# Loads of V, w1 and w2 issued by ScalarE on a second DMA queue, in an attention decode kernel that streams its cache

## Chip, cores, metric

One Trainium2 chip, one core of it. The metric is the device time of one execution in microseconds, as the median of the runs. The hardware profiler gives, for one execution of its own, a span (first to last instruction of the program) and that execution's device time.

## What is computed

One token of a decoder block: pre-LayerNorm attention over a cached K and V with 32 heads, 32,768 positions and a head width of 128, then a pre-LayerNorm dense block with a Mish activation, both with a residual. Everything is in bf16. Cut to what matters:

```python
# x [1,1,512]; k_cache, v_cache [1,32,32768,128]; wq [512,4096]; wo [4096,512]
q = (layernorm(x) @ wq).reshape(1, 1, 32, 128).transpose(0, 2, 1, 3)
p = softmax(einsum("bhqd,bhkd->bhqk", q, k_cache) * 128 ** -0.5)
o = einsum("bhqk,bhkd->bhqd", p, v_cache)
h = x + o.transpose(0, 2, 1, 3).reshape(1, 1, 4096) @ wo
# w1 [512,1376]; b1 [1376]; w2 [1376,512]
a = layernorm(h) @ w1 + b1
out = h + (a * tanh(softplus(a))) @ w2
```

K and V are 268 MB each; all else together is 11 MB.

## The kernel before

The cache of one head is read in two halves of K and two of V. Each half is one DMA of 4 MB: 128 partitions, and on each of them 128 consecutive positions of 128 numbers (32 KB). They land in `ring`, six slots of 4 MB: slots 0 and 1 for the halves of K, 2 and 3 for those of V, 4 and 5 for wq and wo. Later w1, w2 and the last rows of wo (`WL`) share slot 4. The last half of V, V(31,1), comes in four pieces. At the start the first K goes to V's slots, and the last head's V(31,0) to K's slot 0, as nothing else wants them (`HOMES`, `AFTER`).

A head's K is worked on in groups of eight tiles of 128 positions. PE transposes the eight tiles into PSUM (L539), VectorE copies them to SBUF (L542), and PE multiplies each by the query (L517), up to three groups later. From the 256 columns of scores VectorE takes the maximum (L579), two small matmuls spread it (L585, L590), and ScalarE forms the exponentials with their sum in one instruction (L595, `soft_exp`). Then PE multiplies the 256 tiles of V by them (L564, `pv`) and VectorE scales the result (L574, `oev`).

The heads are pipelined by one: round i does the K of head i and the V of head i - 1. `head(i)` holds both halves of K and the first half of V, with the softmax steps set between; `last(i)` holds the second half of V, the scaling, and `soft_exp(i)`, which has to wait for the last `pv` of head i - 1 because it overwrites the same probabilities. PE and VectorE run the rounds as a loop on the chip; ScalarE's and SP's instructions are written out. After the rounds `mid` multiplies 31 heads by wo, does the last head's V, and the second LayerNorm and the dense block follow; both LayerNorms and the Mish use ScalarE for a logarithm and exponentials (L487, L489, L687).

`S.step(engine, ...)` adds an instruction with its semaphore waits to one engine's program, `S.wait` a wait alone, `S.dma` the issue of a DMA. Each engine's program is the order of these calls. All loads but those of x (ScalarE's queue) and b1 (POOL's queue) are in SP's program, in one list:

```python
order = [WQ] + halves("k", 0) + [WO]
for h in range(1, H):
    order += halves("k", h) + halves("v", h - 1)
order += [WL] + halves("v", H - 1) + W1P + W2P
```

For each of them SP waits until the slot's former content is used (`freed_by`: for K when its last tile is transposed, for V when its last matmul is done) and issues the DMA (L418), which adds 16 to a semaphore (`ready`) as it lands. PE waits for that semaphore ahead of a half's first tile. w1 and w2 wait for nothing.

Of the kernel before, what the change touches and what calls it, by code (L numbers as in the profile page):

```python
# [13 lines left out]
PE, ACT, DVE, POOL, SP = "pe", "act", "dve", "pool", "sp"  # L14
# [224 lines left out]
def build_kernel(nc, A_x, A_k_cache, A_v_cache, A_wq, A_wo, B_w1, B_b1, B_w2, out):  # L239
# [102 lines left out]
    W1P = [("w1", 0)]  # L342
    W2P = [("w2", n) for n in range(3)]
# [3 lines left out]
    def halves(kind, h):  # L347
        return [(kind, h, half) for half in range(HALVES)]

    order = [WQ] + halves("k", 0) + [WO]  # L350
# [19 lines left out]
    def slot_of(what):  # L370
        if what in HOMES:
            return HOMES[what]
        if what[0] in ("w1", "w2"):
            return HOMES[WL]
        return what[2] + (HALVES if what[0] == "v" else 0)
# [11 lines left out]
    def free_name(what):  # L387
        return "free" + "_".join(map(str, what))

    def freed_by(what):  # L390
        if what[0] in ("w1", "w2"):
            return []
        if what in AFTER:
            return [free_name(x) for x in AFTER[what]]
        return [free_name((what[0], what[1] - 1, what[2]))]
# [13 lines left out]
    def program(S):  # L409
        t_ = nc.tensor  # L410
        a = nc.scalar
        v = nc.vector
        g = nc.gpsimd
        sp = nc.sync


        def start(dst, src, s):
            S.dma(SP, lambda: sp.dma_start(dst, src).then_inc(s, 16))  # L418

        for what in order:  # L420
            slot = slot_of(what)
            S.wait(SP, freed_by(what))
            flat = ring[:, slot, :]
            if what[0] == "wq":
                start(wq_v, A_wq.rearrange("(k p) n -> p k n", k=KC), ready[slot])
            elif what[0] == "wo":
                start(flat, A_wo.rearrange("(p j) n -> p (j n)", j=32), ready[slot])
            elif what == WL:
                start(wol_v, A_wo[(H - 1) * Dh:H * Dh, :], s_wl)
            elif what[0] == "w1":  # L430
                start(w1_v, B_w1.rearrange("(k p) n -> p k n", k=KC), w1_sems[what[1]])
            elif what[0] == "w2":
                n = what[1]
                if n + 1 < len(W2_J):
                    j0, j1 = W2_J[n], W2_J[n + 1]
                    start(w2_v[:, j0:j1, :], B_w2[j0 * 128:j1 * 128, :].rearrange("(j p) n -> p j n", p=128), w2_sems[n])
                else:
                    start(w2_v[0:FLAST, FJ, :], B_w2[FJ * 128:F, :], w2_sems[n])
            else:
                kind, h, half = what  # L440
                cache = A_k_cache if kind == "k" else A_v_cache
                rows = cache[0, h, half * 128 * TPS:(half + 1) * 128 * TPS, :].rearrange("(p r) d -> p (r d)", r=TPS)
                if what == LASTV:
                    at = 0
                    for n, s in zip(TAIL, [ready[slot]] + piece_sems):
                        start(flat[:, at * Dh:(at + n) * Dh], rows[:, at * Dh:(at + n) * Dh], s)
                        at += n
                    assert at == TPS
                else:
                    start(flat, rows, ready[slot])  # L450
        S.dma(SP, lambda: sp.dma_start(out[0, 0, :].rearrange("(c m) -> c m", c=KC), outr[0:128:32, :]).then_inc(s_out, 16),
              waits=["fin"])
        S.wait(SP, [(s_out, 16)])
# [70 lines left out]
        def k_group(h, half, gi):  # L524
            what = ("k", h, half)
            bg = count[0]
            count[0] += 1
            kt = tiles_of(what)
            tb = T_b[bg % NT]
            for r in range(GT):  # L530
                waits = []
                if r == 0:
                    if gi == 0:
                        waits.append(ready_wait(what))
                    waits.append("identb")
                names = []
                if r == GT - 1:
                    names = [f"trb{bg}"] + ([free_name(what)] if gi == GPS - 1 else [])
                S.step(PE, lambda r=r: t_.matmul(tb[:, r * 128:(r + 1) * 128], kt[:, gi * GT + r, :], identb[:, :],  # L539
                                                 is_transpose=True, start=True, stop=True),  # L540
                       name=(names or None), waits=waits, kind=f"tr{bg % (2 * GPS)}")
            S.step(DVE, lambda: v.tensor_copy(ering[:, bg % NE, :, :].rearrange("p r d -> p (r d)"), tb[:, :]),  # L542
                   name=f"ev{bg}", waits=[f"trb{bg}"],
                   kind=f"ev{bg % (2 * GPS)}")
            pend.append((h, half * TPS + gi * GT, bg))
            flush(KEEP)


        def pv(h, half, r0, r1):
            what = ("v", h, half)  # L550
            vt = tiles_of(what)
            for r in range(r0, r1):
                col = half * TPS + r
                waits = []
                if col == 0:
                    waits.append(f"exp{h}")
                if r == 0:
                    waits.append(ready_wait(what))
                elif half == HALVES - 1 and r in starts:
                    S.in_final(PE, (piece_sems[starts.index(r) - 1], 16))  # L560
                names = []
                if r == TPS - 1:
                    names = [free_name(what)] + ([f"pv{h}"] if half == HALVES - 1 else [])
                S.step(PE, lambda r=r, col=col: t_.matmul(o_ps[:, 0:1], vt[:, r, :], pbuf[:, col:col + 1],  # L564
                                                          start=(col == 0), stop=(col == SCOLS - 1)),
                       name=(names or None), waits=waits, kind="pv" if half == HALVES - 1 else "fv")
# [3 lines left out]
        def oev(h):  # L570
            def out_column():
                return oL[:, :] if h == H - 1 else oT[:, bass.ds(S.index(h), 1)]

            S.step(DVE, lambda: v.tensor_tensor(out_column(), o_ps[:, 0:1], rtotc[:, :], ALU.mult),  # L574
                   name=f"oev{h}", waits=[f"pv{h}", f"rcp{h}"], kind="oev")
# [18 lines left out]
        def soft_exp(h):  # L594
            S.step(ACT, lambda: a.activation(pbuf[:, :], S_ps[:, 0:SCOLS], ACTF.Exp,  # L595
                                             bias=nb[:, :], scale=SC, accum_out=esum[:, :]),
                   name=f"exp{h}", waits=[f"nb{h}"] + ([f"pv{h - 1}"] if h >= 1 else []), kind="exp")
# [6 lines left out]
        def keys(h, half, after=None):  # L604
            for gi in range(GPS):
                k_group(h, half, gi)
                if after is not None and gi == 4:
                    after()


        keys(0, 0)
        keys(0, 1)
        flush(0)
# [16 lines left out]
        def last(i):  # L630
            t = i - 1
            pv(t, 1, 0, TPS)
            oev(t)
            if t < H - 1:
                soft_exp(i)

        def project(j):
            for c in range(KC):
                first = j == 0 and c == 0
                S.step(PE, lambda c=c, first=first: t_.matmul(  # L640
                    yps[:, c:c + 1], wo_v[:, j, c * 128:(c + 1) * 128], oX[:, j:j + 1],
                    start=first, stop=False, skip_group_check=True),
                    waits=(["oX", ready_wait(("wo",))] if first else ()))

        def project_last():
            for c in range(KC):
                S.step(PE, lambda c=c: t_.matmul(yps[:, c:c + 1], wol_v[:, c * 128:(c + 1) * 128], oL[:, :],
                                                 start=False, stop=(c == KC - 1), skip_group_check=True),
                       name=("y" if c == KC - 1 else None), waits=([f"oev{H - 1}", ready_wait(WL)] if c == 0 else ()))

        def mid():
# [12 lines left out]
            pv(H - 1, 0, 0, TPS)  # L664

        S.rounds(1, H, head, last, mid)
        project_last()
        S.step(DVE, lambda: v.tensor_tensor(lnx[:, 1, 0, :], yps[:, 0:KC], lnx[:, 0, 0, :], ALU.add), name="lnh1", waits=["y"])
        layernorm(1)
# [3 lines left out]
        for c in range(KC):  # L673
            S.step(PE, lambda c=c: t_.matmul(y2_ps[32 * c:32 * c + 1, :], lnx[:, 1, 0, c:c + 1], ident[:, :],
                                             start=True, stop=False, skip_group_check=True),
                   waits=(["lnh1", f"exp{H - 1}"] if c == 0 else ()))
        for j in range(FJ + 1):
            for kc in range(KC):
# [4 lines left out]
                    start=False, stop=last, skip_group_check=True),  # L683
# [9 lines left out]
        for j in range(FJ + 1):  # L693
            W = 128 if j < FJ else FLAST
            for c in range(KC):
# [3 lines left out]
                    start=False, stop=(j == FJ), skip_group_check=True),  # L699
# [46 lines left out]
```

## Time and profile before

| | |
|---|---|
| median of 3 runs | 1285.98 us (1285.85 to 1286.2) |
| the profiled execution: device time, span | 1285.47 us, 1283.6 us |
| mean granted clock of PE in it | 0.768 |
| busy share of PE, VectorE, ScalarE | 79%, 56%, 2% |
| DMA: moved, mean rate | 548.48 MB, 427 GB/s |
| time to landing, median: halves of K, of V | 26.6 us, 31.5 us |

Busy shares are of the span. Queues are numbered: q1 is SP's, q10 ScalarE's, q0 POOL's; q8 and q14 fetch instructions. In the timeline and the chain of waits, "SPq" is the sequencer of SP (its issues), "PE hlp L600" the instruction of line 600 that writes the tile `hlp`, and "issue" time in which an engine waited for nothing that the profile shows. "xN" joins N instructions; the length beside it runs from the start of the first to the end of the last. The time to landing runs from the issue of a DMA to the semaphore's update.

### The profile page before, as it was taken

To read this page: it belongs to the slowest core of one execution; us is meant where nothing else is said; L and a number is where in the kernel's file an instruction comes from. 1 tells how busy PE (TensorE), PEld (TensorE's weight loads), DVE (VectorE), ACT (ScalarE), POOL (GpSimd) and SP (SyncE) were. 2 spreads that over 40 slices of the span, in tenths; PEclk is the share of its full clock that TensorE was granted. 3 is DMA by queue.
4 is the path that set the end of the run, shared out by engine and by line. 5 is a ranking of instruction groups with operands and counts; after the bars stand their busy time and mean duration, and the time that the engine had idled before them with its cause. 6 is when DMAs were issued, how large, how long until landed. Compare 5 with 4: busy or idle time off the path is not lost.

```text
span 1283.6 us, 52407 instructions
## 1 busy us (share of the span) xinstructions
PE 1011.0 (79%) x25135; PEld 988.0 (77%) x25135; DVE 712.5 (56%) x1247; ACT 20.6 (2%) x70; POOL 2.3 (0%) x9
## 2 busy tenths in 40 slices
PE   3779877779877779877788877798777798777795
PEld 3779877779777778777788877788777797777795
DVE  2656664456654456654466644466544566544561
ACT  0000000000000000000000000000000000000000
POOL 0000000000000000000000000000000000000000
PEclk9878876778876788777688777788777788767785
DMA  9999999999999999999999999999999999999997
GB/s 405 425 425 436 428 436 429 433 433 428 436 429 434 430 432 434 428 435 430 435 429 432 433 428 434 431 434 432 428 436 428 434 431 432 434 429 435 428 431 294
DMA packets 21730, 548.48 MB, mean 427 GB/s; under 512 B 2288, under 2 KB 3792, under 8 KB 4560
## 3 DMA queue, kind: packets, MB, share of 16 engines
q1 hardware_dynamic: 21640, 548.22, 99.5%
q8 instruction: 14, 0.23, 0.1%
q14 instruction: 4, 0.03, 0.0%
q0 software_dynamic: 64, 0.00, 0.0%
q10 hardware_dynamic: 8, 0.00, 0.0%
HBM read 548.21 MB, written 0.00 MB: 427 GB/s over the span
## 4 chain that ended last, share of the span: by engine, by line
DMA 81%; PE 14%; DVE 2%; issue 2%; ACT 0%; SPq 0%; DVEq 0%
DMA ring<-in_A_v_cache_dram 79%; PE ops L564 10%; PE tps L539 3%; DVE ering L542 2%; DMA ring<-in_A_k_cache_dram 2%; PE sps L517 1%; PE yps L640 0%; PE hlp L585 0%; PE hlp L590 0%; PE sps L681 0%; PE tps L697 0%; PE hlp L600 0%; PE hlp L482 0%; SPq L418 0%; DVE pmax L579 0%
## 5 line engine op out<-in xcount | busy, mean ns | idle before, releaser
L539 PE MATMUL tps<-identb,ring 128*128 128x128 bf16 x8192 | 667.7, 232 | 190.9 <-DMA ring<-in_A_k_cache_dram 184.4
L542 DVE COPY ering<-tps 128x1024 bf16<-128x1024 bf16 x1024 | 669.4, 691 | 247.0 <-PE tps L539 238.1
L539 PEld LDWEIGHTS tps<-identb,ring 128*128 128x128 bf16 x8192 | 524.9, 104 | 194.3 <-DMA ring<-in_A_k_cache_dram 186.9
L517 PE MATMUL sps<-qcur,ering 128*128 128x1 bf16 x8192 | 343.4, 164 | 8.9 <-DVE ering L542 7.8
L517 PEld LDWEIGHTS sps<-qcur,ering 128*128 128x128 bf16 x8192 | 309.3, 97 | 12.0 <-DVE ering L542 10.8
L564 PEld LDWEIGHTS ops<-pbuf,ring 128*128 128x128 bf16 x8192 | 223.0, 102 | 60.8 <-DMA ring<-in_A_v_cache_dram 42.5
L564 PE MATMUL ops<-pbuf,ring 128*128 128x1 bf16 x8192 | 230.4, 165 | 47.4 <-DMA ring<-in_A_v_cache_dram 40.1
L574 DVE TENSOR_TENSOR oT<-ops,rtotc 128x1 f32 x31 | 5.0, 161 | 151.5 <-PE ops L564 151.5
L592 DVE TENSOR_SCALAR nbias<-hlp 128x1 f32<-128x1 f32 x32 | 5.1, 158 | 66.5 <-PE hlp L590 66.5
L587 DVE TENSOR_REDUCE gmax<-hlp 1x1 f32<-1x128 f32 x32 | 8.9, 278 | 49.1 <-PE hlp L585 49.1
L595 ACT ACTIVATE pbuf<-sps,nbias 128x256 bf16<-128x256 f32 x32 | 15.2, 475 | 1231.3 <-PE ops L564 1183.0
L579 DVE TENSOR_REDUCE pmax<-sps 128x1 f32<-128x256 f32 x32 | 13.6, 424 | 15.6 <-PE sps L517 15.6
L590 PE MATMUL hlp<-gmax,onesmat 1*128 1x1 f32 x64 | 18.5, 356 | 0.4 <-DVE gmax L587 0.4
L590 PEld LDWEIGHTS hlp<-gmax,onesmat 1*128 1x128 f32 x64 | 15.8, 304 | 1.3 <-DVE gmax L587 0.9
L585 PE MATMUL hlp<-ident,pmax 128*1 128x128 f32 x64 | 16.1, 344 | 0.5 <-DVE pmax L579 0.5
L600 PE MATMUL hlp<-esum,onesmat 128*128 128x1 f32 x64 | 13.9, 287 | 0.0
L600 PEld LDWEIGHTS hlp<-esum,onesmat 128*128 128x128 f32 x64 | 11.9, 234 | 0.0
L497 PE MATMUL hlp<-xnT,ring 128*128 128x1 bf16 x128 | 3.5, 165 | 9.7 <-DMA ring<-in_A_wq_dram 9.7
L497 PEld LDWEIGHTS hlp<-xnT,ring 128*128 128x128 bf16 x128 | 3.5, 104 | 9.8 <-issue 9.8
L602 DVE RECIPROCAL rtotc<-hlp 128x1 f32<-128x1 f32 x32 | 5.1, 160 | 9.4 <-PE hlp L600 9.4
L640 PE MATMUL yps<-oX,ring 128*128 128x1 bf16 x128 | 3.7, 165 | 5.4 <-issue 5.1
L640 PEld LDWEIGHTS yps<-oX,ring 128*128 128x128 bf16 x128 | 3.6, 104 | 5.6 <-issue 5.2
(61 smaller groups left out, 35.1 us busy)
## 6 DMA issues: line engine op xcount, KB each, us to landing
ring<-in_A_k_cache_dram SPq DMA_DIRECT2D x64, 4096.0 KB, 26.6
ring<-in_A_v_cache_dram SPq DMA_DIRECT2D x63, 4096.0 KB, 31.5
ring<-in_A_wq_dram SPq DMA_DIRECT2D x1, 4096.0 KB, 12.4
ring<-in_A_wo_dram SPq DMA_DIRECT2D x1, 4096.0 KB, 41.3
ring<-in_A_v_cache_dram SPq DMA_DIRECT2D x1, 2048.0 KB, 11.3
ring<-in_B_w_dram SPq DMA_DIRECT2D x1, 1376.0 KB, 18.1
ring<-in_B_w_dram SPq DMA_DIRECT2D x2, 640.0 KB, 19.9
ring<-in_A_v_cache_dram SPq DMA_DIRECT2D x1, 1024.0 KB, 13.4
```

Source lines behind the costliest of these rows:

```text
L497: S.step(PE, lambda h=h, kc=kc: t_.matmul(Q_REG[:, h:h + 1], wq_v[:, kc, h * Dh:(h + 1) * Dh], xnT[:, 0, kc:kc + 1], start=(kc == 0), stop ...
L517: S.step(PE, lambda r=r: t_.matmul(S_ps[:, col0 + r:col0 + r + 1], ering[:, bg % NE, r, :], qcur[:, :], start=True, stop=True), name=(name ...
L539: S.step(PE, lambda r=r: t_.matmul(tb[:, r * 128:(r + 1) * 128], kt[:, gi * GT + r, :], identb[:, :], is_transpose=True, start=True, stop= ...
L542: S.step(DVE, lambda: v.tensor_copy(ering[:, bg % NE, :, :].rearrange("p r d -> p (r d)"), tb[:, :]), name=f"ev{bg}", waits=[f"trb{bg}"], ...
L564: S.step(PE, lambda r=r, col=col: t_.matmul(o_ps[:, 0:1], vt[:, r, :], pbuf[:, col:col + 1], start=(col == 0), stop=(col == SCOLS - 1)), n ...
L579: S.step(DVE, lambda: v.tensor_reduce(pmax[:, :], S_ps[:, 0:SCOLS], AXX, ALU.max), name=f"pmax{h}", waits=[f"qkh{h}"], kind="pmax")
L585: S.step(PE, lambda: t_.matmul(A_REG, pmax[:, :], ident[:, :], start=True, stop=True), name=f"A{h}", waits=[f"pmax{h}", "ident"], kind="A")
L587: S.step(DVE, lambda: v.tensor_reduce(gmax[:, :], A_REG, AXX, ALU.max), name=f"gmax{h}", waits=[f"A{h}"], kind="gmax")
L590: S.step(PE, lambda: t_.matmul(B_REG, onesm[0:1, :], gmax[:, :], start=True, stop=True), name=f"B{h}", waits=[f"gmax{h}", "consts0"], kind ...
L595: S.step(ACT, lambda: a.activation(pbuf[:, :], S_ps[:, 0:SCOLS], ACTF.Exp, bias=nb[:, :], scale=SC, accum_out=esum[:, :]), name=f"exp{h}", ...
L600: S.step(PE, lambda: t_.matmul(C_REG, onesm[:, :], esum[:, :], start=True, stop=True), name=f"C{h}", waits=[f"exp{h}"], kind="C")
L640: S.step(PE, lambda c=c, first=first: t_.matmul(yps[:, c:c + 1], wo_v[:, j, c * 128:(c + 1) * 128], oX[:, j:j + 1], start=first, stop=Fals ...
```

## The change

`start` and the body of the loop become a function `load(eng, what)`, which puts the same wait and the same issue into the program of the engine that is named. SP loads wq, K, wo and WL. V, w1 and w2 are loaded by ScalarE, at places in its program:

```diff
-        def start(dst, src, s):
-            S.dma(SP, lambda: sp.dma_start(dst, src).then_inc(s, 16))
-
-        for what in order:
+        def load(eng, what):
+            def start(dst, src, s):
+                S.dma(eng, lambda: (sp if eng == SP else a).dma_start(dst, src).then_inc(s, 16))
+
             slot = slot_of(what)
-            S.wait(SP, freed_by(what))
+            S.wait(eng, freed_by(what))
...
+        for what in order:
+            if what[0] not in ("v", "w1", "w2"):
+                load(SP, what)
...
+        for what in halves("v", 0):
+            load(ACT, what)
         keys(0, 0)
...
             pv(t, 1, 0, TPS)
             oev(t)
             if t < H - 1:
+                load(ACT, ("v", i, 0))
                 soft_exp(i)
+                load(ACT, ("v", i, 1))
...
         S.rounds(1, H, head, last, mid)
+        for what in W1P + W2P:
+            load(ACT, what)
         project_last()
```

The loads, their sizes, their slots and their waits are the same as before. ScalarE issues both halves of V(0) ahead of its first exponential. In round i it issues V(i,0) ahead of `soft_exp(i)` and V(i,1) behind it, in the last round too; there V(31,1) is four issues. w1 and w2 follow them, ahead of the second LayerNorm's logarithm.

## The prediction

> **What bounds the kernel now.** I read the page first, then the windows view over the middle of the run.
>
> ```profile
> span 1283.6 us, 52407 instructions
> DMA  9999999999999999999999999999999999999997
> GB/s 405 425 425 436 428 436 429 433 433 428 436 429 434 430 432 434 428 435 430 435 429 432 433 428 434 431 434 432 428 436 428 434 431 432 434 429 435 428 431 294
> q1 hardware_dynamic: 21640, 548.22, 99.5%
> q10 hardware_dynamic: 8, 0.00, 0.0%
> DMA 81%; PE 14%; DVE 2%; issue 2%; ACT 0%; SPq 0%; DVEq 0%
> ...
> 637.70:676.56 38.86, 31.18 (x774) 30.67 (x774) 22.11 (x38) 0.57 (x2) 0.00 (x0) 0.76 1.00 432
> ```
>
> One queue (q1, SP's) keeps the 16 DMA engines busy for 99.5% of the span, and nothing but the last slice falls below 405 GB/s. One head's round is 38.86 us at 432 GB/s with a DMA share of 1.00. It moves four halves of 4 MB (two of K, two of V), so one transfer takes T = 38.86 / 4 = 9.72 us. The 8 packets of q10 are those of the only load that ScalarE issues now, so its queue is a second one beside q1.
>
> The timeline of that round (start, length, engine, line) shows how far the engines are behind the transfers.
>
> ```profile
> 637.74 3.59 PE L539 MATMUL tps<-identb,ring 128*128 128x128 bf16 x32 [6.13 <-DMA ring<-in_A_k_cache_dram]
> 649.88 10.67 SPq L418 DMA_DIRECT2D ring<-in_A_k_cache_dram  x2
> 665.07 5.74 SPq L418 DMA_DIRECT2D ring<-in_A_v_cache_dram  x2
> 666.88 3.57 PE L564 MATMUL ops<-pbuf,ring 128*128 128x1 bf16 x128 [1.33 <-DMA ring<-in_A_v_cache_dram]
> 670.55 0.47 ACT L595 ACTIVATE pbuf<-sps,nbias 128x256 bf16<-128x256 f32 x1 [38.28 <-PE ops L564]
> ```
>
> PE starts a head's K at 637.74. The first half is consumed 12.14 us later (SP can refill its slot at 649.88); the second issue of that row is 10.67 less one issue's 0.33 later, so a second half costs 10.34. V half 0 is free 27.33 us after the start. PE waits 6.13 us for K and 1.33 for V half 1, so its own work is 38.86 - 7.46 = 31.4 us per round: 7.5 us of slack, DMA the bound. The middle can't get shorter than its bytes allow; what the change can move is the order in which they land, and with it the two ends of the run.
>
> **The end of the run.** Landings are the issue time (SP's timeline) plus the time to landing (the DMA view on a window of that one issue); the rows of that view come in the order K half 0 and 1 of head 31, V half 0 and 1 of head 30. Below them stand PE's row of the last half of V(30) and pieces of the chain of waits behind it.
>
> ```profile
> 1193.39 10.67 SPq L418 DMA_DIRECT2D ring<-in_A_k_cache_dram  x2
> 1208.82 6.01 SPq L418 DMA_DIRECT2D ring<-in_A_v_cache_dram  x2
> 1233.13 22.02 SPq L418 DMA_DIRECT2D ring<-in_A_v_cache_dram  x5
> ...
> ring<-in_A_k_cache_dram SPq DMA_DIRECT2D x1, 4096.0 KB, 27.2
> ring<-in_A_k_cache_dram SPq DMA_DIRECT2D x1, 4096.0 KB, 26.6
> ring<-in_A_v_cache_dram SPq DMA_DIRECT2D x1, 4096.0 KB, 31.2
> ring<-in_A_v_cache_dram SPq DMA_DIRECT2D x1, 4096.0 KB, 35.2
> ...
> 1249.80 3.57 PE L564 MATMUL ops<-pbuf,ring 128*128 128x1 bf16 x128 [1.02 <-DMA ring<-in_A_v_cache_dram]
> ...
> 1255.18 5.11 issue
> 1266.52 7.04 PE ops L564 x254
> 1275.79 0.30 ACT lns L487
> 1276.70 1.56 PE sps L681 x44
> 1281.23 0.29 DVE outr L702
> ```
>
> K(31) lands at 1220.6 and 1230.3, V(30) at 1240.0 and 1249.7. PE starts the last half of V(30) as it lands (1249.80, after a wait of 1.02) and ends it at 1253.4; from there the chain of waits holds PE, DVE and issue, and no transfer: the span ends 30.2 us later. So the end is set by the moment E at which pv(30) is done, now 1253.4.
>
> **The change, part by part.**
>
> *Issues on ScalarE.* The 64 V halves (67 instructions) and four weight loads leave SP. One issue takes 0.33 us on SP, 0.56 on ACT by its one row:
>
> ```profile
> 0.74 0.56 ACTq L456 DMA_DIRECT2D xr<-in_A_x_dram  x1
> L418 SPq DMA_DIRECT2D ring<-in_B_w_dram x4: 434/517/13855, 1255.2 to 1256.8; - x4
> ```
>
> V(i,0) is issued ahead of exp(i), at +27.33, while exp can't begin before PE's last V matmul at about +32.7: 5.4 us of cover. V(i,1) comes behind exp (0.47 and its accumulator read), some 0.7 us later than SP would; it isn't needed for a round. Both cost nothing. The wait for the slot of V(i,0) holds back only exp(i), whose own data come later. At the end one weight load held SP for 13.86 us, until 1270.65; on ACT it would hold back Ln (1275.79), which leaves 5.1 us of cover: zero, and 5 us of margin.
>
> *SP is not held by V.* Now K(i+1,0) stands behind V(i-1) in one queue. After, it begins as soon as K(i,0) is consumed, beside V(i-1). The engines have to divide themselves. How, is seen best where another queue ran beside q1: POOL's bias load (window 5.9 to 7.9), and code fetches (window 13 to 24.2).
>
> ```profile
> q1 hardware_dynamic: 106, 0.87, 102.8%
> q0 software_dynamic: 64, 0.00, 2.1%
> ...
> q1 hardware_dynamic: 159, 4.69, 97.2%
> q8 instruction: 1, 0.02, 0.6%
> ```
>
> In 2 us, q0 got 64 packets through beside 106 of q1, in the middle of a 4 MB load, and q1's share stayed full: packets of two queues go turn by turn, and a turn costs no visible time. I take equal shares and no loss.
>
> *The steady rounds.* With equal shares, one K and one V transfer run as a pair and both land after 2T = 19.43 us: K(i+1,0) with V(i-1,1), then K(i+1,1) with V(i,0). Let a pair (K(i,0), V(i-2,1)) land at L. PE does V half 1 until L+3.6, K half 0 until L+15.7, waits for K half 1 at L+19.4, ends it at L+29.8 to 31.6, is done with V half 0 4.85 us later (27.33 - 12.14 - 10.34), at L+34.6 to 36.5, and waits for V half 1 at L+38.86. Every slot is refilled before its queue is empty (the tightest, V half 0, by over 2 us), so the DMA stays full and a round stays 38.86 us. PE's wait moves from K half 0 to K half 1. Gain and loss here: 0.
>
> *The start.* Rows for WQ, K(0,1) and K(1,1), then SP's timeline from the first load on (WQ; K(0); K(1); V(0)):
>
> ```profile
> ring<-in_A_wq_dram SPq DMA_DIRECT2D x1, 4096.0 KB, 12.4
> ring<-in_A_k_cache_dram SPq DMA_DIRECT2D x1, 4096.0 KB, 32.0
> ring<-in_A_k_cache_dram SPq DMA_DIRECT2D x1, 4096.0 KB, 59.6
> ...
> 0.75 0.47 SPq L418 DMA_DIRECT2D ring<-in_A_wq_dram  x1
> 1.28 0.95 SPq L418 DMA_DIRECT2D ring<-in_A_k_cache_dram  x2
> ...
> 2.80 1.13 SPq L418 DMA_DIRECT2D ring<-in_A_k_cache_dram  x2
> 36.04 13.83 SPq L418 DMA_DIRECT2D ring<-in_A_v_cache_dram  x2
> ```
>
> A load into an empty queue lands after 12.4 us, 2.7 more than T. K(1,1), issued at 3.4, lands at 63.0, so WO and K(1,0) at about 43.6 and 53.3. After the change V(0,0) joins at 36.0 + 2.7 = 38.7. WO has 4.9 us of work left and lands at 48.4; V(0,0), half done, at 58.1; K(1,0) at 67.9; V(0,1) at 77.6; K(1,1), alone for its last half, at 82.4. PE consumes K(1,0) by 67.9 + 12.1 = 80.0, in time for K(2,0) to follow at 82.4 and land at 92.2, and K(1,1) by 82.4 + 10.3 = 92.8. Only then can K(2,1) be issued, and both V slots are full and unread: the queues are empty. K(2,1) lands at 92.8 + 12.4 = 105.2 at the latest instead of 101.9. Idle: 1 us if a load starts at once, 3.3 by the WQ row. I take 2.5, as 12.4 holds a first ramp. Afterwards both queues stay full.
>
> *The end.* The bytes before the pair (K(31,0), V(29,1)) are those that have landed at 1220.6 now, so L = 1220.6 + 2.5 = 1223.1. Today K(31,1) has the next 9.72 us of DMA to itself; after the change it shares with V(30,0) and lands at L + 19.4 = 1242.5, not 1230.3. PE is done with K(31,0) at about 1239 and waits. Half 1 takes 10.3 without a wait, 12.1 after one; I take 11.2, so 1253.7. Today the same point is 1233.13 + 10.34 = 1243.5, and E follows 9.9 later, 1.0 of which is the wait for V(30,1), which lands at 1252.2 and so is no longer waited for: E = 1253.7 + 8.9 = 1262.6, 9.2 us later than now. V(31,1) is issued after exp(31), at 1263.3, with its queue empty since 1261.9; it lands by 1263.3 + 12.4 = 1275.7. PE wants its first piece at E + 13.1 + 3.5 = 1279.2 and the last at about 1282, so that idle time is hidden by PE's own chain (3.5 us to spare). The two weights (2.8 MB at 432 GB/s, 6.5 us) land by 1282.2 and are wanted from E + 23.3 = 1285.9: hidden. The held issue ends now 1.5 us after V(31,1), which two transfers behind V(30,1) lands at 1269.1; so ACT is free at about 1277.2, and Ln is due at E + 22.4 = 1285.0: hidden.
>
> **Sum.** Issues 0, rounds 0, start 2.5 (carried into L), end 6.7: +9.2 us. The profiled execution took 1285.47 us, 1.9 over its span and 0.5 below the median of 1285.98. Against the median: 1285.98 + 9.2 = 1295.2, said as 1295. Bounds: start 1 to 3.3, K half 1 10.3 to 12.1, and an offset inside the pairs of up to 3 us, which moves K(31,1) by half, 1.5: own range 1291 to 1299.
>
> **Rivals.**
>
> *Whole transfers take turns* (0.10). If a queue keeps an engine for its whole share of a load, a pair lands one after the other. K first: K(31,1) lands at L + 9.7, PE goes through without a wait (31.4 from L + 3.6), E = L + 35.0 where today it is 1220.6 + 32.8, so 2.2 later plus the start. V first: as my forecast, less a little. 1288 to 1294. Against it: the 64 packets of q0 that went through in 2 us of a running load. The Trainium skill, "DMA: Bandwidth & Descriptors", Queues, rings and completion order, has an engine drain a whole packet of about 9 to 17 descriptors from one ring before it switches, which would be this rival; q0's row (64 packets beside 106) speaks against it.
>
> *Each turn costs time* (0.10). K(0,1) was issued at 1.8 and landed at 33.8, WQ at 0.75 + 12.4 = 13.15; the two K halves took 20.65 us instead of 19.43, with a 16 KB fetch of q8 between: 1.2 us for 0.6 us of bytes (an engine moves 432 / 16 = 27 GB/s), so up to 0.3 per change of queue. K and V change at every packet: some 32 per engine and round, times 31 rounds, times 0.3 = 300 us, 1585. A hundredth of that is 3 us, so it decides from a few ns on. Against it the q0 row.
>
> *No slower: the loads are served in the order of their issue* (0.07). Then K and V land as today, start and end included: 1286. For it: the issue order hardly changes. Against it: q0 did not wait behind the 24 MB queued on q1.
>
> *Two queues carry more* (0.07). The mean is 432 GB/s, the best slices of the page 436: 0.9% of 31 rounds (1205 us) is 11 us: 1295.2 - 11 = 1284 at best, 1290 half way. It draws level with today at 0.76%. For it: nothing in the rows. The Trainium skill, the same page, Where 436 GB/s comes from, puts the ceiling at 435; the measured 432 leaves 0.7% by it.
>
> **How the numbers follow.** Forecast 0.66: 1295. The range 1287 to 1305 takes in its own range, the whole transfers, half of the higher rate, and turns that cost up to 5 ns (5 us); outside are no change and costly turns. A measurement can tell about 0.2% (2.6 us) from no change. Slower by more: the forecast, most of the whole transfers, the costly turns, a little of the higher rate, 0.81. Within: no change, most of the higher rate, the low end of whole transfers, 0.13. Faster: 0.06.
>
> **What would show it.** Right: q10 with about half the bytes; DMA share 1.00 and 432 GB/s in the middle; K halves landing 23 and 27 us after their issue, V halves 22 and 35, each 19.4 after the last of its queue; PE's wait for K moved to half 1 of each head, near 4 us, and one for V half 1 of 2 to 3; DMA idle near 92 to 95; pv(30) done near 1262. Wrong: fewer GB/s in the middle (a turn costs), K halves 9.7 apart (whole transfers), or ScalarE late for exp.

## The result, and the profile after

| | before | after |
|---|---|---|
| median | 1286.09 us (1285.85 to 1286.2, 4 runs) | 1298.41 us (1296.52 to 1299.02, 4 runs) |
| profiled execution: device time, span | 1285.47, 1283.6 us | 1298.69, 1296.8 us |

The run list of before has one run more here than above. The ratio of the means is 1.0093, with a 95% interval of 1.008 to 1.0106: by the medians slower by 12.3 us, where 9.2 were forecast and 1287 to 1305 us was the range. The page of the kernel after:

```profile
span 1296.8 us, 52407 instructions
DMA  9989999999999999999999999999999999999995
GB/s 403 423 359 425 432 437 430 429 436 434 427 434 437 427 431 436 432 427 437 433 427 435 436 428 431 436 431 428 437 432 428 435 435 430 430 436 431 428 410 218
```

Two slices stand out: the third (65 to 97 us, 359 GB/s) and the last (218, where before it was 294). Between them the rate is that of before, but for the last slice but one (410, before 431). The windows view (length; busy time of PE, PEld, DVE, ACT, POOL with counts; PE clock; DMA share; GB/s) says the same for one round of the middle and for the hole in the third slice:

```profile
637.70:676.56 38.86, 30.11 (x683) 29.75 (x681) 21.58 (x35) 0.56 (x2) 0.00 (x0) 0.74 1.00 432
90.00:95.00 5.00, 5.00 (x129) 5.00 (x126) 5.00 (x9) 0.00 (x0) 0.00 (x0) 1.00 0.23 95
95.00:100.00 5.00, 4.67 (x159) 4.23 (x156) 1.69 (x5) 0.00 (x0) 0.00 (x0) 0.81 0.84 315
```

432 GB/s and a share of 1.00 with two queues, as with one: no cost of a turn shows, and no gain. In the hole PE works almost without a gap (5.00 and 4.67 of 5 us), VectorE without one in the first 5 us, and the DMA engines do not: 0.77 and 0.16 of 5 us, together 4.65 us, they are idle. Now the end. The timeline's issues of V(29,1) and of K(31,0) and K(31,1):

```profile
1190.57 0.33 ACTq L419 DMA_DIRECT2D ring<-in_A_v_cache_dram  x1
1202.03 13.98 SPq L419 DMA_DIRECT2D ring<-in_A_k_cache_dram  x2
```

The DMA view for each of them alone, in the order K(31,0), K(31,1), V(29,1); the last number is the time to landing:

```profile
ring<-in_A_k_cache_dram SPq DMA_DIRECT2D x1, 4096.0 KB, 22.9
ring<-in_A_k_cache_dram SPq DMA_DIRECT2D x1, 4096.0 KB, 28.7
ring<-in_A_v_cache_dram ACTq DMA_DIRECT2D x1, 4096.0 KB, 36.4
```

PE's timeline from K(31,1) on:

```profile
1244.44 0.62 PE L543 MATMUL tps<-identb,ring 128*128 128x128 bf16 x8 [1.75 <-DMA ring<-in_A_k_cache_dram]
1257.05 1.75 PE L568 MATMUL ops<-pbuf,ring 128*128 128x1 bf16 x64
1261.55 3.57 PE L568 MATMUL ops<-pbuf,ring 128*128 128x1 bf16 x128
```

And pieces of the chain of waits behind pv(30):

```profile
1266.94 5.65 issue
1276.72 2.65 issue
1279.37 7.04 PE ops L568 x254
```

K(31,0) lands at 1224.9 and V(29,1) at 1227.0, nearly a pair; K(31,1), issued at 1215.7, lands at 1244.4, 19.5 us behind K(31,0), where before the two were 9.7 apart. PE has waited for it, works on it until V begins at 1257.05, and ends pv(30) at 1265.1 without a wait for V: 11.7 us later than before (1253.4). The chain behind it takes 31.7 us instead of 30.2; 1.1 of that lies in its two longest stretches of "issue" (5.65 and 2.65; before 5.11 and 2.10). One packet of q8, which fetches instructions, falls into each of the four, so they are likely waits for code; that is not shown. 11.7 + 1.5 = 13.2 us, the difference of the two spans.

### The profile page after: what moved, and what is told of

The parts are those of the page before. It is cut to its first block, busy times and chain, and to the rows that moved or that the text cites. A ratio compares the mean times of both kernels' runs of the same rounds, so it can differ in the third digit from the quotient of the medians.

```text
span 1296.8 us, 52407 instructions
## 1 busy us (share of the span) xinstructions
PE 1057.1 (82%) x25135; PEld 1033.2 (80%) x25135; DVE 719.7 (55%) x1247; ACT 20.6 (2%) x70; POOL 2.3 (0%) x9
## 4 chain that ended last, share of the span: by engine, by line
DMA 62%; PE 33%; DVE 2%; issue 2%; another core or an unknown queue 1%; ACT 0%; SPq 0%; DVEq 0%
DMA ring<-in_A_k_cache_dram 62%; PE tps L543 24%; PE sps L521 7%; PE ops L568 2%; DVE ering L546 1%; PE yps L648 0%; PE hlp L594 0%; PE sps L691 0%; PE hlp L589 0%; PE tps L707 0%; PE hlp L604 0%; PE hlp L486 0%; SPq L419 0%; DVE pmax L583 0%
## 5 line engine op out<-in xcount | busy, mean ns | idle before, releaser
L543 PE MATMUL tps<-identb,ring 128*128 128x128 bf16 x8192 | 711.2, 242 | 115.6 <-DMA ring<-in_A_k_cache_dram 106.2
L546 DVE COPY ering<-tps 128x1024 bf16<-128x1024 bf16 x1024 | 676.5, 692 | 211.3 <-PE tps L543 207.9
L543 PEld LDWEIGHTS tps<-identb,ring 128*128 128x128 bf16 x8192 | 558.8, 109 | 121.3 <-DMA ring<-in_A_k_cache_dram 108.9
L521 PE MATMUL sps<-qcur,ering 128*128 128x1 bf16 x8192 | 349.3, 165 | 6.6 <-DVE ering L546 6.6
L521 PEld LDWEIGHTS sps<-qcur,ering 128*128 128x128 bf16 x8192 | 320.4, 99 | 9.4 <-DVE ering L546 9.4
L604 PEld LDWEIGHTS hlp<-esum,onesmat 128*128 128x128 f32 x64 | 11.6, 227 | 0.0
```

The costliest lines, as they stand in the source:

```text
L521: S.step(PE, lambda r=r: t_.matmul(S_ps[:, col0 + r:col0 + r + 1], ering[:, bg % NE, r, :], qcur[:, :], start=True, stop=True), name=(name ...
L604: S.step(PE, lambda: t_.matmul(C_REG, onesm[:, :], esum[:, :], start=True, stop=True), name=f"C{h}", waits=[f"exp{h}"], kind="C")
```

## The experiments

The theory: the bytes, the rate and the rounds stay the same, and the time comes from what lands when, at two places. Where the second queue starts, the first halves of V take half of the engines from the K that PE needs next; then they lie unread, all slots are full or in use, and the engines run out of work (the entry). At the end K(31,1) shares with V(30,0), and PE's last chain starts later (the tail). The rivals: a price for each issue on ScalarE, or for each turn of two queues, spread over the run.

**All loads on ScalarE.**

The first six loads go out behind that of x; later ones stand in the rounds:

```diff
-        for what in order:
-            if what[0] not in ("v", "w1", "w2"):
-                load(SP, what)
...
+        for what in order[:6]:
+            load(ACT, what)
...
+                for what in (halves("k", i + 1) if i + 1 < H else [WL]):
+                    load(ACT, what)
                 load(ACT, ("v", i, 0))
                 soft_exp(i)
                 load(ACT, ("v", i, 1))
```

> ScalarE issues every load, in the order of before (the half V(i,1) behind the exponential); SP issues the output alone. Order theory: one queue, one order, so as before: 1286, at most +1 as the first load goes out behind that of x. Rival, ScalarE pays for issuing (its exponential or logarithm late, or its queue slower): twice as many issues as in the change, so at least the 12 us of it, 1298 or more.

Measured: 1286.42 us against 1285.86, ratio 1.0003 (0.9993 to 1.0013). The page of this kernel shows that ScalarE's queue moves all bytes and stays as full:

```profile
q10 hardware_dynamic: 21640, 548.22, 99.4%
```

So neither ScalarE as the issuer nor its queue costs anything that can be measured (the interval ends at 1.7 us); it takes two queues side by side.

**Only a part of V on ScalarE.** The edit is the condition that picks the loads, in three kernels. SP issues the loads for which it is false, and at ScalarE's places the same condition lets through those for which it is true (these lines are left out here):

```diff
-            if what[0] not in ("v", "w1", "w2"):
+            if not on_act(what):
...
# v0_only:      what[0] == "v" and what[1] == 0
# middle_only:  what[0] == "v" and 3 <= what[1] <= 27
# tail_only:    what[0] in ("w1", "w2") or (what[0] == "v" and what[1] >= 28)
```

> Only V(0,0) and V(0,1) are issued by ScalarE; all else stays on SP, in the order of before. Order theory (the time comes from what lands when at the two ends): the queues run empty once, after K(2,0) has landed, as with all of V on ScalarE, where the first 11 loads landed 5.2 us later than before; afterwards one queue again. So +5 us, 1291. Rival, a price per issue on ScalarE or per turn of two queues: 2 of 64 halves, so 1286.

> V(3) to V(27) are issued by ScalarE, the first three and the last four heads and w1, w2 by SP. Order theory: two queues share in 25 of 31 rounds, but both stay full, so nothing is lost there and the ends are those of before: 1286 to 1288. Rival, a price per issue or turn spread over the run: 25/31 of the 12.3 us, 1296.

> V(28) to V(31), w1 and w2 are issued by ScalarE, all else by SP. Order theory: no empty queue at the start; K(31,1) shares with V(30,0) and lands late, PE's chain behind it is as long as with all of V on ScalarE: 12.3 less the 5.2 of the start, +7 us, 1293. Rival, a price spread over the run: 4 of 32 heads, 1287 to 1288.

Measured, against 1285.86: v0_only 1291.31 (ratio 1.004, 1.0025 to 1.0054), middle_only 1290.85 (1.0042, 1.0026 to 1.0059), tail_only 1299.49 (1.0107, 1.009 to 1.0124). The first was as the theory had it. The other two were 3 and 6.5 us above it. Their rivals missed too: middle_only is 5 us below its rival, though it has 25 heads on two queues and costs the same as v0_only with one; tail_only is over 11 us above its rival. The windows of middle_only, then of tail_only, show what I had missed:

```profile
205.00:210.00 5.00, 5.00 (x127) 5.00 (x125) 5.00 (x8) 0.00 (x0) 0.00 (x0) 1.00 0.46 197
210.00:215.00 5.00, 4.79 (x150) 4.46 (x145) 3.17 (x7) 0.00 (x0) 0.00 (x0) 1.00 0.47 144
```

```profile
1175.00:1180.00 5.00, 5.00 (x117) 5.00 (x115) 4.41 (x7) 0.00 (x0) 0.00 (x0) 0.90 0.72 308
1180.00:1185.00 5.00, 4.79 (x141) 4.70 (x139) 4.55 (x9) 0.00 (x0) 0.00 (x0) 1.00 0.38 118
```

The hole of about 5 us is not one of the start. It comes some 50 us after the first V on the second queue, wherever that is: near 93 us with head 0, 209 with head 3, 1180 with head 28. It comes only once: in the change and in these three kernels every other stretch of 5 us between 60 and 1260 us has a DMA share of 0.93 or more, but for the one next to the two of tail_only (0.85). PE is busy through nearly all of it. Middle_only pays the entry and nothing else, so leaving the two queues is free; tail_only pays the entry and the tail.

**The first V behind the first exponential.** With the entry understood, it can be avoided: the two loads of V(0) go out later, at about the time when K(1,0) lands (at 52.7 and 53.2 us in the trace).

```diff
-        for what in halves("v", 0):
-            load(ACT, what)
         keys(0, 0)
...
         soft_exp(0)
+        for what in halves("v", 0):
+            load(ACT, what)
```

> The change, with the two loads of V(0) behind the first exponential instead of ahead of it (issued at 53.6 us rather than 37 and 51). Entry theory (the queues run empty once, as the first V halves take half of the engines from the K that PE needs next, and then lie unread): K(1,0) lands at 53 as before, K(1,1) at about 70, as PE wants it, and no slot is left full and unread, so about 5 us come back: 1293 to 1294. Rival, the 5 us are a price of starting a second queue, wherever its first load stands: no difference, 1298.

Measured: 1294.38 us against 1286.0, ratio 1.0065 (1.0051 to 1.0079), 4 us below the change, of the "about 5" that were expected; its five runs spread over 3.1 us. The hole is gone:

```profile
90.00:95.00 5.00, 0.85 (x9) 0.76 (x9) 0.16 (x1) 0.00 (x0) 0.00 (x0) 0.50 0.98 416
95.00:100.00 5.00, 3.22 (x115) 3.17 (x116) 0.00 (x0) 0.00 (x0) 0.00 (x0) 0.50 1.02 436
```

**And the tail back on SP.** The same, with `on_act` true for V(0) to V(27) alone.

> As v0_behind_exp, and V(28) to V(31), w1 and w2 go back to SP: 28 of 32 heads run on two queues. Entry and tail theory: both costs are gone, 1286 to 1287. Rival, two queues cost something per round: 1291 or more, as middle_only.

Measured: 1286.2 us, ratio 1.0001 (0.9992 to 1.001). Two queues side by side over 28 of 32 heads, and nothing is lost that these runs could show (the interval ends at 1.3 us): the cost lies at the two places.

**Only V(30) on ScalarE.** `on_act` is `what[0] == "v" and what[1] == H - 2`.

> Only V(30,0) and V(30,1) are issued by ScalarE. Tail theory (PE's chain to the end starts when K(31) and V(30) are worked off): V(30,0) is issued at 1209, when K(31,0) has its turn, and takes half of its share; K(31,0) lands at 1230 instead of 1220.6, K(31,1) at 1249 instead of 1230.3, pv(30) ends at 1270 instead of 1253.4: +16.5 to 18, 1303, more than with all of V on ScalarE. Rival, a price by the number of heads on two queues: 1286 to 1289.

Measured: 1302.61 us, ratio 1.0125 (1.011 to 1.014): two loads of 64 moved, and more lost than with all of them. The DMA view's rows of K(31,0) and K(31,1), issued at 1193.5 and 1203.8, and PE's timeline:

```profile
ring<-in_A_k_cache_dram SPq DMA_DIRECT2D x1, 4096.0 KB, 35.7
ring<-in_A_k_cache_dram SPq DMA_DIRECT2D x1, 4096.0 KB, 44.8
```

```profile
1229.23 3.59 PE L546 MATMUL tps<-identb,ring 128*128 128x128 bf16 x32 [14.64 <-DMA ring<-in_A_k_cache_dram]
1248.66 1.04 PE L546 MATMUL tps<-identb,ring 128*128 128x128 bf16 x8 [7.47 <-DMA ring<-in_A_k_cache_dram]
1266.35 3.57 PE L571 MATMUL ops<-pbuf,ring 128*128 128x1 bf16 x128
```

K(31,0) lands at 1229.2 and K(31,1) at 1248.6, where 1230 and 1249 were expected, and pv(30) ends at 1269.9 (1270). Two halves of V taken out of the order move both halves of K behind them.

**Only w1 and w2 on ScalarE.** `on_act` is `what[0] in ("w1", "w2")`.

> Only w1 and w2 are issued by ScalarE, from 1254.5 us on, beside V(31) on SP. If turns go by packets: w1 has packets of 2.7 KB, V of 32, 16, 8 and 4 KB, so w1 takes about 3.6 us from V(31,1) over its 32 packets per engine; its last piece lands at 1273.4, where PE wants it at 1273.1: +0.5 to +1, 1286.5. If turns go by bytes: the last piece lands at 1276.3, +3.3, 1289. Rival, ScalarE held by a full queue delays the logarithm of the second LayerNorm: several us more.

Measured: 1286.82 us against 1286.0, ratio 1.0006 (0.9997 to 1.0015), as turns by packets would have it and 2.5 us below turns by bytes. The DMA view has the landing of V(31,1)'s last piece, issued at 1254.9; the timeline PE's wait for it, and ScalarE's issues and logarithm:

```profile
ring<-in_A_v_cache_dram SPq DMA_DIRECT2D x1, 512.0 KB, 18.9
```

```profile
1274.08 0.73 PE L571 MATMUL ops<-pbuf,ring 128*128 128x1 bf16 x16 [0.82 <-DMA ring<-in_A_v_cache_dram]
...
1254.16 16.65 ACTq L419 DMA_DIRECT2D ring<-in_B_w_dram  x3
1277.05 0.29 ACT L494 ACTIVATE lns<-lns,epsc 128x1 f32<-128x1 f32 x1 [22.79 <-DVE lns L492]
```

It lands at 1273.8 (expected 1273.4; 1276.3 by bytes), and PE waits 0.82 us for it. ScalarE is held until 1270.8, 6 us before its logarithm: hidden. How long is a turn? A load of 4 MB has 128 rows of 32 KB, 8 for each DMA engine, and a row is one packet in the profile. Whole loads in turn would have set K(31,0) and V(29,1) of the change 9.7 us apart, and they landed within 2.1. The trace of the change also holds a record of each packet. Joined where one of 32 KB ends and the next begins, the packets of 1000 us in the middle form 16 chains, one for each DMA engine. In them 9,634 of 10,521 stretches on one queue are a single packet long; the longest are 7. So the two queues take turns mostly packet by packet. The Trainium skill, "DMA: Bandwidth & Descriptors", Queues, rings and completion order, has an engine drain a whole packet of typically some 9 to 17 descriptors before it turns to another ring; the trace of this case does not agree, and the measurement decides.

**A version that beats both.** If the end hangs on pv(30), bytes are better placed behind V(30,1) than ahead of it: in the kernel before, the last piece of V(31,1) lands at 1269.8, and PE wants it at about 1273.1, so some 3 us of room is left there. The edit, abridged, is to the kernel before, all loads on SP; the last 8 of wo's 32 row blocks are split off, and PE waits for them on a semaphore of their own (`s_wo2`):

```diff
-    order += [WL] + halves("v", H - 1) + W1P + W2P
+    order += [WL, WO2] + halves("v", H - 1) + W1P + W2P
...
+    start(flat[:, 0:WO_J * D], wo_rows[:, 0:WO_J * D], ready[slot])   # wo, WO_J = 24
+    start(flat[:, WO_J * D:], wo_rows[:, WO_J * D:], s_wo2)           # wo2
```

> The kernel before, all loads on SP, with the last quarter of wo (1 MB, the rows of 8 KB per partition that the last 8 of the 32 products with wo use) loaded behind V(30,1) instead of at the start. Tail theory (the end is set by pv(30), and so by the bytes that have to land ahead of V(30,1); what lands behind it has about 3 us to spare): V(30,1) lands 1 MB, 2.4 us, earlier, the last pieces of V(31) and the weights when they do now: -2.4 us, 1283.6. Rival, the end is set by all bytes together (DMA busy for 99.5%): no difference, 1286.

Measured: 1283.97 us against 1286.05, ratio 0.9983 (0.9974 to 0.9992), 2.1 us faster. PE's last half of V(30) starts 2.24 us earlier than in the kernel before (1249.80), as it lands:

```profile
1247.56 3.57 PE L570 MATMUL ops<-pbuf,ring 128*128 128x1 bf16 x128 [1.34 <-DMA ring<-in_A_v_cache_dram]
```

In the profiled execution 0.8 of it was lost again to longer stretches of "issue" in the chain behind (5.37 and 2.65 us, before 5.11 and 2.10; the span is 1282.2). In the kernel before, the DMA is busy for 99.5% of the span, and still it is not the sum of the bytes that sets the end.

## Why the prediction was right

The time came out in the range, the cost fell at the two places that were named, and for the reasons that were given. The sum was short of it by 3 us, as one of its terms was half of what it should be and one effect was not in it.

**Issues on ScalarE, 0.** Right: all_on_act 1.0003, w_only 1.0006; in the change ScalarE was held by its queue from 1268.3 until 1279.9, and its logarithm came at 1288.6.

**Equal shares, turns without a price, rounds unchanged.** Right: 38.86 us of the middle still move 432 GB/s, v0_behind_exit28 lost nothing that shows, and the last loads took nearly the times to landing that were forecast: K halves 22.9 and 28.7 us (23 and 27 forecast), V(29,1) 36.4 (35). Of PE's waits, only the place was right. It waits for K half 1 and V half 1, but not evenly: between 150 and 1240 us, where it waits, for K half 1 from 1.1 to 5.6 us (near 4 forecast), for V half 1 from 0.4 to 6.3 (2 to 3 forecast); for K(31,1) it waits 1.75 us (3.7 forecast).

**The start, 2.5 us.** The place and the mechanism were right, the size was off. SP's and ScalarE's issues of K(2,0), K(2,1) and V(1,0), from the timeline, and below the DMA view's row for each:

```profile
78.64 0.33 SPq L419 DMA_DIRECT2D ring<-in_A_k_cache_dram  x1
95.22 0.33 SPq L419 DMA_DIRECT2D ring<-in_A_k_cache_dram  x1
103.20 0.33 ACTq L419 DMA_DIRECT2D ring<-in_A_v_cache_dram  x1
```

```profile
ring<-in_A_k_cache_dram SPq DMA_DIRECT2D x1, 4096.0 KB, 14.8
ring<-in_A_k_cache_dram SPq DMA_DIRECT2D x1, 4096.0 KB, 15.7
ring<-in_A_v_cache_dram ACTq DMA_DIRECT2D x1, 4096.0 KB, 15.1
```

K(2,0) landed at 93.4 and K(2,1) was issued at 95.2, where I had 92.8: PE needed 12.4 us for K(1,1) after its wait (it landed at 82.8), and I had taken the 10.3 of a half without one, though I priced the same case at 11.2 in the tail. The first 11 loads were down at 118.3; in the kernel before, V(1,0), the eleventh there, was issued at 89.60 and landed at 113.1, by its row of the DMA view:

```profile
ring<-in_A_v_cache_dram SPq DMA_DIRECT2D x1, 4096.0 KB, 23.5
```

So the term is 5.2 us, above my bound of 3.3. (At the low end the working gives 92.8 - 92.2 = 0.6, not the 1 that I wrote.) I also called it a cost of the start; it is one of the entry.

**The tail, 6.7 us.** Right in mechanism and nearly in size. With 5.2 in place of 2.5, L is 1225.8; K(31,1) lands at 1244.4 rather than L + 19.4 = 1245.2, as K runs 2 us ahead of V in the pairs; PE needs 11.6 us for its half (11.2 was taken): its last transpose ends at 1256.05, 1.0 us ahead of V's start. V goes as said. That gives pv(30) at 1265.1; the two misses, 0.8 early and 0.4 late, cancel in part. The idle time ahead of V(31,1) and the late weights were hidden by PE's chain, as said. Not foreseen: 1.1 us more of "issue" in that chain; why is open.

**The sum.** 5.2 + 6.5 (11.7 - 5.2) + 1.5 = 13.2 in the profiled execution; the median moved by 12.3. That 1298.4 still lies inside the narrower own range, 1291 to 1299, is luck: the entry was above its bound, and the 1.5 us of the chain were in no term.

**The rivals.** Whole transfers by turns: out, the loads of a pair land 2 us apart and not 9.7. (The sign I had named for it, halves of K 9.7 apart, was a bad one: by whole transfers they too would be 19.4 apart.) A price per turn, or a higher rate: out, 432 GB/s. Order of issue: out for two queues. K(31,1) was issued 5 us ahead of V(30,0), and by order it would have landed some 9.7 us behind V(29,1), near 1236.7; it landed at 1244.4.

Open: the four runs of the change spread over 2.5 us, those of before over 0.35. The offset between K and V in the pairs is not fixed, as PE's uneven waits above show, and where the last pair stands in it moves the tail: PE waits 1.75 us for K(31,1) in the change, 2.96 in v0_behind_exp and 7.13 in tail_only. So the split of the cost is known only roughly. The tail is 7.1 us by the total of the change and 8.4 by that of tail_only (each less 5.2 for the entry), and 8.4 by that of v0_behind_exp, which has no entry. The entry is 5.2 us by the landings in the change, 5.0 and 5.5 by the totals of middle_only and v0_only, and 4 by the difference of the change and v0_behind_exp. No run here shows that the offset differs from execution to execution.

## What to carry to other kernels

A single queue is also an order: loads come down in the order in which they are wanted. A second queue on the same busy engines added no bandwidth here; it hands half of it to loads that are wanted later, which is harmless while every slot is refilled in time, and costs where slots run out (at the entry) or where the work behind the last loads is the end of the program. In a kernel that is bound by DMA, look for the load from which the last chain of the compute engines starts, and put whatever it does not need behind it.

## What the runs showed of the hardware

- Two hardware queues on the same 16 engines, each with packets of 32 KB, gave 432 GB/s, the same as one queue.
- Turns go by packets and not by bytes, mostly one packet at a time (9,634 of 10,521 stretches in 1000 us of the change): beside V, w1 and w2 moved V's last piece by 4 us (1273.8 against 1269.8) and not by 6.5.
- A DMA issue can hold its engine, and not by the number of loads alone: in w_only the last three weight loads held ScalarE for 16.65 us, the first of the held ones being the third of that queue, behind loads of 512 and 640 rows; at the start of the change six loads of 4 MB, the first of 512 rows and five of 128, go out in some 0.5 us each. What sets the hold was not tested.
- In this kernel two halves of V that leave the order cost more than all 64: 16.6 us in v30_only against 12.3.
